# A written-out order of 3128 jobs is replaced by another one

## The chip, the cores and the metric

The kernel runs on one core of one Trainium2 chip. The metric is the device time of one execution in microseconds (us); a kernel's figure is the median of several runs. One further execution was recorded by the hardware profiler, and all rows below come from that one. A core has five engines with queues of their own that are worked off in order: TensorE (PE in the rows; PEld is its weight load), VectorE (DVE), ScalarE (ACT), GpSimd (POOL) and SyncE (SP), which here issues nearly all transfers. All transfers that SP issues run on the same 16 DMA engines.

## The reference

Eight batches, eight heads, 576 positions, 64 numbers per head. Rotary embedding on q and k, softmax attention, and then a gated feed-forward stage on the attention's output x (8 x 576 x 512):

```python
q_rot, k_rot = (rotate(q), rotate(k))
scores = scale * np.matmul(q_rot, k_rot.transpose(0, 1, 3, 2))
scores = scores - np.max(scores, axis=-1, keepdims=True)
attn = np.exp(scores)
attn = attn / (np.sum(attn, axis=-1, keepdims=True) + 1e-09)
x = np.matmul(attn, v)            # then heads side by side: B, S, 512
...
for k in range(5):
    gate_pre += conv_w[k][None, None, :] * xp[:, k:k + S, :]   # xp: x behind 4 zero rows
gate = 1.0 / (1.0 + np.exp(-gate_pre))
val = x @ w_val
return (gate * val @ w_out).astype(np.float32)
```

## The kernel before

Two heads form a pair, so there are 32 pairs, p = 0 to 31, and four pairs make a batch. Products of full precision are made of three TensorE products of rounded parts: a high part `hi` and a rest `lo` (hi*hi, hi*lo, lo*hi). A pair goes through these steps, each of which is one or several jobs:

- `load`, `load_v`: SP brings q (`qin`), k (`kin`) and v from memory. `qin` and `kin` exist once, so the next pair's load waits until the pair ahead has been turned into `q` and `k`.
- `rope_mul`, `rope_add` (DVE or POOL), `qk_hi`, `qk_lo`: the rotation and the two parts. For pair 0 alone the addition is done by TensorE (`rope_mm`, L314), with the identity and a swap matrix as weights.
- `s_mm` (L364), `s_mix` (L374): scores of 128 query rows into a bank of PSUM. For the first four pairs (`APART`) each head has its own job.
- `s_max` (DVE, L389) and `s_exp` (ACT, L398): the row maximum, and the exponential with the row sum.
- `t_mm` (PE, L384): the probabilities are transposed in blocks of 64; `t_copy` (ACT or DVE, L467, L469) takes them out of PSUM into `pt` and `pr`.
- `r_add`, `r_inv`, `r_copy`, `r_write`, `r_read`: the reciprocal row sums are written to memory (`rd`, L526) and read back spread over all partitions (`rb`, L534, three transfers of 288 KB in all).
- `pv_mm`, `pv_left` (PE, L480, L490): attention times v. `x_norm` (DVE, L538) multiplies the result with `rb`, which gives x.
- `x_hi`, `x_lo`, five `tap`s (L567 to L570) and `gate` (L582): the parts of x, and the gate.
- For each batch `f_mm` (PE, L602) with w_val, then `y_mul`, `y_hi`, `y_lo`, then `f_mm` with w_out, `o_out` (ACT L637 or DVE L638) into one of two places of the buffer `o`, and `o_dma` (SP, L641), which sends 288 KB of it out. The next `o_out` into the same place waits until that transfer has ended.

PSUM has four units (`u`), each of two banks. Every job that starts a new result in PSUM names its unit, and waits until the last reader of what stood there is done.

Nothing is decided while the kernel runs, and nothing by a scheduler when it is built. The function lists the 3128 jobs with the engines that may do each and with what each reads and writes. The text `ORDER` (lines 33 to 158) then names them one after the other: the job's number; behind it V, A or G where it may run on DVE, ACT or POOL; behind a colon the buffers and PSUM units it takes; and with `<` a job that it has to follow. `Plan.run` calls them in that order, and each engine's queue holds its own jobs in that order. `FILLS` (line 159) says at which place of the order a number of transposes of the identity is put in, whose result nobody reads:

```python
            if step in FILLS:                  # L205
                fill(*FILLS[step])
...
    def fill(n, slot):
        bank = psum.tile([128, 2, 512], F32, name="ps_f", tag=f"u{slot}")
        for _ in range(n):
            T.transpose(out=bank[:, 0, 0:128], in_=ident, identity=ident)   # L405
```

Of the kernel before, what the change touches and what calls it, by code (L numbers as in the profile page):

```python
# [33 lines left out]
7 24 8 11 17 0:0 35 10 153 113 229 30V 12V 13V 18V 14:0 19V 31V 20:1 25V 15 26V 9 104 16 32:2 36V 21 140 114A 37G 27:3 22 1 33 115 38:0 28 29 116 45:1  # L34
39 34 23 117 119A 42:3 40 46:0 48:2 43:1 147 142G 47:0 51:0 49:2 44:1 57:1 141V 105A 41 54:3 52:3 50 143G 58:0 53 120V 144A 74:2 55:1 59:2 66:0 145V
56:3 63:1 148V 216 75A:0 72:3 149V 82A:0 76:2 146 150V 73A:0 67<148 64:2 151A 60:3 106 65 152 77A 61:3 160:1 223 218G 68:0 62 163:2 217V 69 83:3 161:1
84A 70 219G 80 71 154:0 162:0 164:2 118 85 165:1 172:1 107 87:0 86A 169:2 81A 88:0 155:3 220A 78:3 224G 173:0 156 170:1 174:2 157:0 221V 171:3 166:1
158:2 292 225G 222 175:2 89:0 159 167:3 121V 168 178:0 226V 79A 131 184:1 2 227V 185A:1 186:3 228 179<2 187A:1 3 176:0 236:1 299 294G 180:1 177 233:3
4 237:2 293G 181 239:2 234:3 194A:1 238:0 230:0 5 182 240:0 235:1 190:1 295V 132A 92:3 231:1 296A 133 90 232 297V 241 93 6 300V 488 377:100 298 301V
110A 91 191A 183 108 188:0 134 302V 197:2 254:1 189A 192 109 195 303V 262:0 198A 193A 490V 255<198 199:1 196A 94 304 263A:0 242:2 256:2 495 489G 378A  # L40
95 251:0 270A:0 257 243:3 111G 245:3 252:1 244:2 248:1 246:0 491G 253:3 315:2 249:2 247 260:0 135 250 379 321:3 316:3 112G 261A:0 266:1 322:1 492A
202:0 258 497V 122 317:0 203 200:1 259 136 323:1 268:2 496V 267A 271 273 312:3 380 275:0 274A 498V 269A 276:0 309:1 201:1 272A 381 383A 264:2 313:0
493G 137A 204 310:2 265A 382 205 560 499A 138V 311 327:2 500 494 314:2 384V 567 306:1 328:3 96A:0 385G 206 123A 307:1 318:3 329 124 368:011 207 308
561G 277:0 324:2 319:2 330:0 210A:1 325:0 562G 320:3 211 305 326 336:3 125 331<211 208A:1 212 278:2 563G 337A:1 213 279 346A:1 369A 569G 214 340:3
564A 332:3 215:0 280 370 98A:1 139V 281 371 333 99 374A 338:0 334 341A 126 372 282 100 375G 339A:1 342:3 335 573 101 343A 347:0 568G 349 283 102 348A
502:23 351:1 350A 352:1 373 103:1 344 503:1 376G 345A 505:2 504:0 353:1 512:10 570V 506:2 513:0 565G 571A 517:23 515:3 514:1 520:1 209G:2 395:013 501
128A 632 356:1 516:3 518:2 354 129V 521 572 519 507:03 127 284A:2 639 357 286A:2 510:0 130G 508:3 355 511 633G 287 509 358 288 396A 530:3 97G:4 359
522:0 531A:0 289 528:1 538V:0 634V 529A:0 523<538 290 635G 574:31 524:1 291:2 566 534:2 577:2 525 641G 575:0 578:0 539:0 536 535V 576:2 526 532:1
285G:0 527 533A 540V 579:32 397 360V:3 541 636A 546:1 580:3 640G 543:0 537A 544:0 547 582:1 581 542V 637V 583 584:03 398 704 362A:2 548 545:0 585:2
361G:1 363 549 586:1 587:0 642G 550 364 588:3 600:0 365 717 643A 426:3 399 427 601A:1 366 706G 428 551 429 367:3 594:0 644 589:12 610A:1 400 638 711  # L50
430<610 401A 590:3 431 705G 595<610 592:1 591 432 433 596:2 593 402G 415:1 434 416 597 606:2 435V 707G 604:0 607A:1 436 417 418 598 605A 403V 646:23
599 713V 708A 611:0 608 613 649:0 419<599 709G 612A 420 615:1 647:3 650:1 421 616:1 422 614V 648:3 712V 860 404:3 405 386:013 609A 423 714G 406 617:1
407 424A 651:20 710 425 715A 408<710 654:1 409 410 652:2 655 411 602:1 862G 653 412 603A 413V 666:0 861G 674:2 414 682A:0 667<682 675A:0 716 661:13
387A 668:0 620:2 867 863G 664:3 669 621 662:1 665:0 388 663:2 656:03 389 552A:4 390 672:1 392A 659:2 618 864A 657:0 660 619 391 673A:0 622 868G 658
718:31 623 670 393G 723:02 719:3 721:1 720:1 865G 724:2 722:3 437:3 671 438 726:0 725 678:1 932 869V 727 873 680:0 683 645 679V 685 870G 676:2 687:0
686A 688:0 439 684V 677A 440 681V 744:1 871V 733:02 745A:1 872 441<871 734:3 442 939 933G 443 736:1 735:0 444 738:1 737:2 934G 445 689:0 446A 728:02
935G 447 739<446 731:2 692:3 729:0 394G 732 690 740:3 730 693 941G 554V:2 741 555 748:0 754A:1 742 556 940G 746:1 749A 691 557 747A:1 558 694 942G
559:4 874:01 695 866 943A 468:2 936V 458:3 877:1 937G 459 743 460 878:1 875:2 461 944 469 876:3 1004 752:1 470 696A:0 1011 626V:0 471 624A:1 462<696
627 757 755 463 758A 628 464 756A 759:1 465 760:1 629 472<758 466A:0 473 630 474 1006G 467 750:3 753V 631:2 761:1 475 938 751V 879:10 697G:4 476A:1
882:0 889:23 477 1005G 880:3 883 890:1 881 900:0 1007G 892:2 891:0 894:1 901V:0 893:2 902:2 1012G 910V:0 903A:0 884:30 895<910 1013G 885:0 762:2 887:3  # L60
886 764 896:1 1014G 698A:3 765 897 699 625G:2 763 1015A 700 888 701 1008A 951:10 702 1009G 766 703:0 954:2 478:3 952:0 1017 955:1 898 479 1076 899 480
# [884 lines left out]
```

## Time and profile before

| | |
|---|---|
| median of 3 runs (lowest, highest) | 695.08 us (694.02, 696.48) |
| the profiled execution | 694.14 us |
| its span, first to last instruction | 692.4 us |
| PE busy | 658.4 us, 95% |
| DVE busy | 572.9 us, 83% |
| ACT busy | 467.0 us, 67% |
| POOL busy | 303.1 us, 44% |
| granted TensorE clock, mean over the span | 0.979 of full speed |
| moved by DMA | 72.85 MB, mean 105 GB/s |

Busy time counts matmuls, arithmetic and copies, not waiting. An engine that is busy for 95% of the span can lose little by waiting, but it can also be busy at half its clock. The granted clock is given as a share of 2.4 GHz; it has two levels, 1.2 and 2.4 GHz. Figures between them are means over a stretch.

### The profile page before, as it was taken

How to read it: one execution, taken by the hardware profiler on the slowest of the kernel's cores; microseconds unless marked ns; L12 is line 12 of the kernel's file. 1: busy time of each engine (PE TensorE's matmuls, PEld its weight loads, DVE VectorE, ACT ScalarE, POOL GpSimd, SP SyncE). 2: the span in 40 equal slices, each digit the busy share in tenths (PEclk: the TensorE clock that was granted, in tenths of full speed). 3: DMA queues.
4: the chain of work that ended last, by engine and by line, in shares of the span. 5: the costliest groups of instructions: out<-in, count | busy, mean ns of one | idle time of the engine just before them, and what ended most of it. 6: DMA issues, size and time to landing. Idle time of an engine off the chain costs nothing. (4 is left out here: it accounts for less than half of the span.)

```text
span 692.4 us, 21271 instructions
## 1 busy us (share of the span) xinstructions
PE 658.4 (95%) x8967; PEld 542.8 (78%) x8967; DVE 572.9 (83%) x868; ACT 467.0 (67%) x1004; POOL 303.1 (44%) x241
## 2 busy tenths in 40 slices
PE   9999899999999989999989998999999999999997
PEld 8877568787888867967877767878779788679796
DVE  5999999999889887887887877688878878888673
ACT  4889988877577776677776666666576654777511
POOL 1325666577533256537325554236555370450000
PEclk9689999999999999999999998999999999999999
DMA  7264434243334222334323323322344232231102
GB/s 237 89 181 142 138 99 141 88 132 110 122 104 142 77 101 88 105 111 138 121 88 108 108 70 104 87 79 84 123 123 138 93 126 68 63 99 37 54 19 69
DMA packets 42721, 72.85 MB, mean 105 GB/s; under 512 B 15449, under 2 KB 18050, under 8 KB 42626
## 3 DMA queue, kind: packets, MB, share of 16 engines
q1 hardware_dynamic: 42082, 70.91, 32.3%
q8 instruction: 70, 1.15, 0.7%
q10 hardware_dynamic: 544, 0.59, 0.3%
q14 instruction: 25, 0.20, 0.1%
HBM read 61.89 MB, written 9.59 MB: 103 GB/s over the span
## 5 line engine op out<-in xcount | busy, mean ns | idle before, releaser
L389 DVE TENSOR_REDUCE nm<-ps_s 128x1 f32<-128x576 f32 x288 | 206.5, 750 | 42.0 <-PE ps_s L364 29.6
L398 ACT ACTIVATE p<-ps_s,nm 128x576 f32<-128x576 f32 x256 | 187.9, 739 | 76.4 <-DVE nm L389 74.1
L364 PE MATMUL ps_s<-k,q 64*128 64x288 f32 x1536 | 155.7, 312 | 8.3 <-ACT o L637 2.9
L364 PEld LDWEIGHTS ps_s<-k,q 64*128 64x128 f32 x1536 | 129.0, 191 | 31.4 <-ACT p L398 8.8
L480 PE MATMUL ps_a<-pt,v 128*64 128x256 f32 (+1 forms) x1024 | 137.3, 412 | 2.2 <-ACT p L398 0.6
L301 POOL TENSOR_TENSOR kin<-kin,tab 128x576 f32<-128x576 f32 x49 | 70.7, 1452 | 131.7 <-DMA kin<-in_k 99.1
L467 ACT COPY pt<-ps_t 128x1024 f32<-128x1024 f32 (+1 forms) x119 | 110.5, 945 | 24.4 <-PE ps_t L384 22.9
L602 PE MATMUL ps_f<-y,wout_hi 64*128 64x288 f32 (+2 forms) x1024 | 110.7, 302 | 3.8 <-DVE x L538 1.9
L567 DVE SCALAR_TENSOR_TENSOR ps_c<-x,cw,ps_c 128x576 f32<-128x576 f32 (+2 forms) x132 | 105.7, 802 | 5.7 <-ACT ps_c L570 2.0
L480 PEld LDWEIGHTS ps_a<-pt,v 128*64 128x64 f32 x1024 | 69.0, 137 | 49.5 <-issue 4.8
L384 PE MATMUL ps_t<-ident,p 64*128 64x64 f32 x2172 | 97.9, 229 | 6.8 <-ACT p L398 2.9
L384 PEld LDWEIGHTS ps_t<-ident,p 64*128 64x128 f32 x2172 | 87.4, 141 | 20.5 <-ACT p L398 8.3
L602 PEld LDWEIGHTS ps_f<-y,wout_hi 64*128 64x128 f32 x1024 | 83.8, 185 | 10.0 <-DVE x L538 2.8
L301 POOL TENSOR_TENSOR qin<-qin,tab 128x640 f32<-128x640 f32 (+1 forms) x43 | 65.8, 1537 | 57.9 <-DVE nm L389 23.5
L602 PE MATMUL ps_f<-xh,wval_hi 64*128 64x288 f32 (+2 forms) x512 | 86.5, 316 | 3.5 <-ACT p L398 1.5
L602 PE MATMUL ps_f<-xh,wval_lo 64*128 64x288 f32 (+2 forms) x512 | 81.0, 294 | 0.0
L602 PE MATMUL ps_f<-xl,wval_hi 64*128 64x288 f32 (+2 forms) x512 | 80.9, 294 | 0.0
L602 PE MATMUL ps_f<-y,wout_lo 64*128 64x288 f32 (+2 forms) x512 | 79.2, 291 | 0.0
L602 PEld LDWEIGHTS ps_f<-xh,wval_hi 64*128 64x128 f32 x512 | 53.8, 187 | 8.2 <-ACT p L398 2.3
L336 POOL TENSOR_TENSOR k<-kin,k 128x576 fp32r<-128x576 f32 x26 | 37.0, 1423 | 52.0 <-ACT k L327 17.5
L552 POOL TENSOR_TENSOR xl<-x,xh 128x576 fp32r<-128x576 f32 (+1 forms) x26 | 36.4, 1400 | 46.3 <-ACT xh L546 32.2
L602 PEld LDWEIGHTS ps_f<-xl,wval_hi 64*128 64x128 f32 x512 | 53.8, 187 | 0.0
(108 smaller groups left out, 922.5 us busy)
## 6 DMA issues: line engine op xcount, KB each, us to landing
kin<-in_k SPq DMA_DIRECT2D x31, 576.0 KB
qin<-in_q SPq DMA_DIRECT2D x31, 512.0 KB
v<-in_v SPq DMA_DIRECT2D x32, 320.0 KB
out_t<-o SPq DMA_DIRECT2D x28, 288.0 KB
rb<-rd SPq DMA_DIRECT2D x31, 144.0 KB
rb<-rd SPq DMA_DIRECT2D x31, 128.0 KB
wst<-in_w_val SPq DMA_DIRECT2D x4, 512.0 KB
o<-in_w_out SPq DMA_DIRECT2D x4, 512.0 KB
```

The source lines that it names most:

```text
L301: return eng.tensor_tensor(out=t[:, i, a:b], in0=t[:, 0 if p < RAW else i, a:b], in1=table[:, i, a:b], op=ALU.mult)
L336: return eng.tensor_tensor(out=lo, in0=rotated(p, n, a, b), in1=hi.bitcast(F32), op=ALU.subtract)
L364: T.matmul(out=tiles[h][:, half, 0:288], lhsT=st["q"][HEAD[h], x, c * 128:c * 128 + 128], rhs=st["k"][HEAD[h], y, k0 + half * 288:k0 + hal ...
L384: T.transpose(out=bank[0:src.shape[1], x, k * D:(k + 1) * D], in_=src[rows], identity=ident[rows, rows])
L389: return V.tensor_reduce(out=st[f"nm{i}"], in_=st[f"s{i}"], axis=AX.XY, op=ALU.max, negate=True)
L398: return A.activation(out=to.rearrange("p (b x) -> p b x", b=2), in_=st[f"s{i}"], func=AF.Exp, bias=st[f"nm{i}"], scale=1.0, accum_out=sum ...
L467: return A.copy(out=dst, in_=src)
L480: T.matmul(out=st[f"a{g}"][HEAD[h], 0:n], lhsT=st["v"][:, j, h, :], rhs=st[f"pt{g}"][:, h * 4 + j], start=(j == 0), stop=False)
L552: return eng.tensor_tensor(out=st["xl"][:, a:b], in0=xs[p % NX][:, 4 + a:4 + b], in1=st["xh"][:, a:b].bitcast(F32), op=ALU.subtract)
L567: return V.scalar_tensor_tensor(out=acc, in0=x_sb, scalar=w, in1=acc, op0=ALU.mult, op1=ALU.add)
L602: inst = T.matmul(out=acc[:, x, 0:hi - lo], lhsT=wt[w][HEAD[h], kc, dc * 128:(dc + 1) * 128], rhs=mv[HEAD[h], lo:hi], start=(turn == 0 and ...
```

## The change

The table `ORDER` is replaced by another one, and `FILLS` with it. Jobs, buffers, arithmetic and number of transfers are the same; the place of nearly every job in the order, the engine of some jobs that have a choice, and many buffer and PSUM unit numbers differ. The new table comes from a planner that let transfers queue behind each other. The identity transposes at the start are 20, not 50, and stand three places earlier in the order.

```diff
 ORDER = """
-7 24 8 11 17 0:0 35 10 153 113 229 30V 12V 13V 18V 14:0 19V 31V 20:1 25V 15 26V 9 104 16 32:2 36V 21 140 114A 37G 27:3 22 1 33 115 38:0 28 29 116 45:1
...
 """
-FILLS = {15: (50, 0)}
+FILLS = {12: (20, 0)}
```

How often a step that has a choice runs on which engine, before and after: `t_copy` on DVE 72 and 64 (ACT 184 and 192), `rope_mul` on POOL 92 and 92, `qk_lo` on POOL 26 and 21 (DVE 41 and 46), `tap` on DVE 146 and 143 (ACT 19 and 22), `y_hi` on DVE 15 and 11 (ACT 21 and 25), `x_hi` on DVE 11 and 14 (ACT 22 and 19), `weight_step` on POOL 9 and 14 (DVE 39 and 36).

Three places of the queues show what moves. The first is TensorE's queue behind the identity transposes and the rotation of pair 0, where `ps_s` are scores, `ps_t` transposed probabilities and `p` the probabilities; before:

```order
L364 MATMUL ps_s<-k_71,q_73 128x288 x36
L384 MATMUL ps_t<-ident,p 128x64 x16
L384 MATMUL ps_s<-ident,p 128x64 x4
L374 MATMUL ps_s<-k_71,q_73 128x288 x6
L364 MATMUL ps_s<-k_71,q_73 128x288 x6
```

and TensorE's queue at the same place now:

```order
L364 MATMUL ps_s<-k_71,q_73 128x288 x48
L384 MATMUL ps_s<-ident,p 128x64 x4
L374 MATMUL ps_s<-k_71,q_73 128x288 x6
L384 MATMUL ps_t<-ident,p 128x64 x16
L374 MATMUL ps_s<-k_71,q_73 128x288 x6
```

All 48 score matmuls of the first pair's four query tiles now stand ahead of its first transposes, where 36 did.

The second place is DVE's first work on pair 0, the products of `qin` and `kin` with the table `tab` (L301) and the rests `k` (L336) and `q` (L333); before:

```order
L301 TENSOR_TENSOR qin<-qin,tab 128x256
L301 TENSOR_TENSOR kin<-kin,tab 128x288 x4
L301 TENSOR_TENSOR qin<-qin,tab 128x256
L301 TENSOR_TENSOR qin<-qin,tab 128x128 x2
L336 TENSOR_TENSOR k_71<-ps_r,k_71 128x288
L301 TENSOR_TENSOR qin<-qin,tab 128x256
L336 TENSOR_TENSOR k_71<-ps_r,k_71 128x288
```

and DVE's queue at the same place now:

```order
L301 TENSOR_TENSOR kin<-kin,tab 128x288 x3
L301 TENSOR_TENSOR qin<-qin,tab 128x128
L301 TENSOR_TENSOR kin<-kin,tab 128x288
L301 TENSOR_TENSOR qin<-qin,tab 128x128
L301 TENSOR_TENSOR qin<-qin,tab 128x256 x4
L657 TENSOR_SCALAR o<-o 128x20
L333 SCALAR_TENSOR_TENSOR q_73<-ps_r,q_73 128x128
L660 TENSOR_SCALAR o<-o 128x20
L661 SCALAR_TENSOR_TENSOR o<-o 128x20
L336 TENSOR_TENSOR k_71<-ps_r,k_71 128x288 x2
```

DVE now makes all ten products (one of them was POOL's) before the first rest, and those of `kin` come first.

The third place is SP's queue of transfers around the loads of pair 23, where batch 3 leaves through `out_t`; before:

```order
L293 DMA qin<-in_q 128x2x512
L293 DMA qin<-in_q 64x2x64 x2
L289 DMA kin<-in_k 128x1152
L641 DMA out_t<-o 128x576
L526 DMA rd<-rr 9x128
L641 DMA out_t<-o 128x576
L293 DMA qin<-in_q 128x2x512
L293 DMA qin<-in_q 64x2x64 x2
L289 DMA kin<-in_k 128x1152
L534 DMA rb<-rd 64x576
```

and SP's queue at the same place now:

```order
L293 DMA qin<-in_q 128x2x512
L293 DMA qin<-in_q 64x2x64 x2
L641 DMA out_t<-o 128x576
L289 DMA kin<-in_k 128x1152
L297 DMA v_75<-in_v 128x640
L526 DMA rd<-rr 9x128
L293 DMA qin<-in_q 128x2x512
L293 DMA qin<-in_q 64x2x64 x2
L526 DMA rd<-rr 9x128
L289 DMA kin<-in_k 128x1152
L297 DMA v_76<-in_v 128x640
L534 DMA rb<-rd 64x576
```

The first output now stands ahead of the load of `kin`, not behind it.

## Rows read from the trace of the kernel before

**Rows 1.** The page: busy time by engine, and TensorE's clock in 40 slices.
```profile
PE 658.4 (95%) x8967; PEld 542.8 (78%) x8967; DVE 572.9 (83%) x868; ACT 467.0 (67%) x1004; POOL 303.1 (44%) x241
...
PEclk9689999999999999999999998999999999999999
```

**Rows 2.** Windows: length, busy PE, PEld, DVE, ACT, POOL, then clock, DMA share, GB/s.
```profile
0.00:20.00 20.00, 17.81 (x128) 16.01 (x130) 12.51 (x33) 9.64 (x24) 4.25 (x9) 0.97 0.70 221
20.00:40.00 20.00, 19.24 (x182) 18.38 (x180) 17.35 (x29) 16.39 (x38) 6.12 (x5) 0.60 0.42 117
...
80.00:100.00 20.00, 17.22 (x212) 12.75 (x214) 19.95 (x30) 17.09 (x38) 13.60 (x11) 0.93 0.41 125
```

**Rows 3.** Timeline of PE: start, duration, work, [wait ahead of it and its end].
```profile
245.74 0.34 PE L384 MATMUL ps_s<-ident,p 64*128 64x64 f32 x4 [1.02 <-DVE o L638]
...
267.28 0.53 PE L602 MATMUL ps_f<-y,wout_hi 64*128 64x288 f32 x4 [1.15 <-DVE x L538]
...
351.80 1.06 PE L364 MATMUL ps_s<-k,q 64*128 64x288 f32 x12 [0.82 <-DVE x L538]
...
413.60 0.71 PE L384 MATMUL ps_t<-ident,p 64*128 64x64 f32 x16 [0.74 <-DVE x L538]
...
429.07 1.81 PE L364 MATMUL ps_s<-k,q 64*128 64x288 f32 x11 [2.94 <-ACT o L637]
...
452.03 3.02 PE L480 MATMUL ps_a<-pt,v 128*64 128x256 f32 x24 [0.60 <-DVE x L538]
...
497.04 0.54 PE L602 MATMUL ps_f<-y,wout_hi 64*128 64x288 f32 x4 [0.79 <-DVE x L538]
```

**Rows 4.** Timeline of SP and ACT from 418 us, around the longest wait.
```profile
418.62 2.69 SPq L293 DMA_DIRECT2D qin<-in_q  x3
...
421.36 0.59 SPq L289 DMA_DIRECT2D kin<-in_k  x1
...
421.99 0.43 SPq L641 DMA_DIRECT2D out_t<-o  x1
...
428.37 0.65 ACT L637 ACTIVATE o<-ps_f 128x576 f32<-128x576 f32 x1 [2.69 <-DMA out_t<-o]
```

**Rows 5.** Windows with the columns of rows 2: stretches at the slow clock.
```profile
19.38:26.20 6.82, 6.82 (x71) 6.80 (x68) 5.91 (x10) 6.17 (x13) 0.53 (x1) 0.55 0.26 86
...
29.62:39.86 10.24, 10.24 (x98) 9.77 (x98) 8.50 (x14) 7.81 (x19) 3.46 (x3) 0.53 0.41 106
...
428.98:435.80 6.82, 6.73 (x62) 6.73 (x64) 1.77 (x3) 3.12 (x10) 5.96 (x5) 0.55 0.13 46
```

**Rows 6.** Timeline from 402 us: row sums of one pair written, read, used.
```profile
405.31 0.51 SPq L526 DMA_DIRECT2D rd<-rr  x1
...
407.88 1.75 SPq L534 DMA_DIRECT2D rb<-rd  x3
412.79 0.76 DVE L538 TENSOR_TENSOR x<-ps_a,rb 128x576 f32<-128x576 f32 x1 [1.84 <-DMA rb<-rd]
```

**Rows 7.** Timeline of the first 16 us, PE and DVE.
```profile
1.36 7.49 PE L405 MATMUL ps_f<-ident 128*128 128x128 f32 x50 [1.36 <-POOL ident masks.py:199]
...
4.38 0.42 DVE L301 TENSOR_TENSOR qin<-qin,tab 128x256 f32<-128x256 f32 x1 [2.97 <-DMA tab<-in_tab]
...
8.90 0.75 PE L314 MATMUL ps_r<-kin,ident 128*128 128x288 f32 x2
...
10.62 0.46 DVE L336 TENSOR_TENSOR k<-ps_r,k 128x288 fp32r<-128x288 f32 x1 [2.44 <-ACT k L327]
...
13.34 2.60 PE L364 MATMUL ps_s<-k,q 64*128 64x288 f32 x24
```

**Rows 8.** Timeline of the last pair: its attention on PE, its x on DVE.
```profile
656.79 0.76 PE L490 MATMUL ps_a<-pr,v 64*64 64x320 f32 x8
...
658.16 0.42 DVE L538 TENSOR_TENSOR x<-ps_a,rb 128x256 f32<-128x256 f32 x1
```

More of the change, by code (lines that the diff above doesn't have):

```diff
@@ L38 @@
[L38 to L49, printed above, removed]
@@ new lines @@
+1305G 1063 1096:2 1099 927 1065 1097 1306G 928 1066 929 1110:2 930 850:3 1126A:1 851 1067 852 931:1 853 1307V 1238 1111<1126 1100:10 996V:4 1112:0
+997G:3 854<996 1103:1 855 1113 856 1101:3 1104 857 840:2 1308V 1102 841 1070V:0 1309G 842 1315A 858V:1 1120:1 843 1071 1114 1121A 1376 1118:3 1115
+1072 844<1115 1119A:1 1122:1 1073 845 1123A 846 1316 847 1074 1246:31 848A:0 1068A:0 820:2 849 1249:2 821 1075:2 1383 1378G 822 1247:0 1250:1 823
+1248:2 1251:01 1377G 1310 1317 1129:3 824<1310 1252:1 1131:1 825 1130A 1132:1 1379G 826 1254:3 1253 1124 1127 827 1255 1128V 1272:0 828V:0 1125A
@@ new lines @@
+1706:3 1713 1718:2 1831V 1707 1667 1716:3 1719A:1 1824V 1767:01 1825V 1717A:1 1542:2 1770:0 1714 1543 1544 1768:2 1771:0 1545 1832 1769:3 1762:31 1715
+1983 1729:0 1546<1715 1763:1 1731:1 1547 1724 1765:3 1764 1727 1548 1725V 1732:1 1549 1826 1766 1790:3 1728V 1550 1730A 1788:1 1791A:0 1551V 1722:0
+1789A:0 1720:3 1552 1733:1 1723A 1721V 1772:21 1985G 1782:0 1773:0 1553:3 1976 1984G 1775:2 1554 1774:1 1555 1783<1775 1776:2 1556 1986G 1784:1
+1777:21 1798V:0 1785 1557<1798 1780:3 1558 1559 1778:0 1781 1560 1779 1839:01 1561 1786 1734:2 1562A 1977G 1840:2 1736 1563 1841:0 1978G 1842:1
@@ new lines @@
+2333 2605A 2617 2615 2315 2726 2334 2616A 2316A:1 2335 2797V 2610:2 2618A 2619:1 2608:3 2620:1 2611V 2317 2338:0 2609A 2339 2340 2336V:0 2341 2798
+2621:1 2486A:2 2558A:3 2624:1 2487 2625 2488 2864 2805 2622 2489 2337 2623 2559 2871 2626 2560 2342<2558 2490 2343 2627 2491:3 2344 2345 2561 2318:1
+2630A:2 2319 2346V:1 2628A:2 2320 2631 2321 2347 2629G:3 2669:0 2877 2632 2670 2671 2562 2672 2322<2632 2633 2323 2563:0 2324 2634 2325 2872G
+2673<2563 2326V:0 2674 2635:4 2675 2676 2865G 2734:32 2677 2658:1 2678A 2737:0 2659 2660 2679 2738:1 2661 2866V 2739:02 2735:3 2867G 2742:2 2736:2
@@ new lines @@
+2980:0 2995 2977A:1 2974:2 2714<2995 2981A 2975V 2715 2716 2717 2996:1 2986:0 2930V:2 2997:0 2931 2928A:0 3000:1 2998:0 2987A 2929G:1 2932 3002
+2718V:0 3003 2999 2933 3001 2934 3004 2935:0 2719 3005 3006 3010V:0 3008A:1 3009V:2 3007 3011 3016A 3018A:3 3038:2 3039 3040 3041 3024:1 3025 3012
+3026 3017V 3027 3019 3042<3012 3043 3020 3044 3013 3045 3014 3028<3020 3029 3021 3015:2 3030 3022 3052:0 3053 3046 3023 3031 3054 3032 3066:3 3049
+3033A 3055 3050V 3067 3034 3068 3035 3047V 3069 3048 3056<3035 3036V 3057 3037 3058 3051 3092:1 3093 3070<3037 3094 3095 3059 3071 3060 3072 3063
@@ L158 @@
+3061A 3073 3064V 3096<3060 3062 3097 3098 3065 3099 3074 3080:2 3102V:1 3081 3077 3082 3103 3083 3078A 3116:0 3100A:0 3079 3075A 3117 3101 3076
+3084<3075 3085 3086 3087 3118 3088A:1 3119 3089 3104:1 3090V:0 3105 3120<3090 3091 3121 3122 3123 3106 3124A:1 3107 3125 3126A:0 3108<3126 3127 3109
+3110 3111 3112V:1 3113 3114V:0 3115
 """
-FILLS = {15: (50, 0)}
+FILLS = {12: (20, 0)}
 class Plan:
```

216 lines of the change are left out of this document (105 added, 111 removed).

## The prediction

> **What bounds the kernel now.** I read the page's busy times first, then windows of 20 us, then every wait of PE of 0.2 us or more, and then, for the longest of them, what SP had issued ahead. The page says that PE is busy for 658.4 of 692.4 us, so that all its waiting together is 34.0 us, and that its clock falls in a few slices only [rows 1]. So the matmuls set the time, they are the same after the change, and a new order can win three things: waits of PE, slow-clock time, and the two ends of the program. The windows show one exception: from 80 to 100 us DVE is busy for 19.95 of 20 us and PE for 17.22, so the first stretch, in which PE has no work of an earlier batch to fill in, is set by DVE as well [rows 2].
>
> The waits of PE are many and short. Seven of them lead back to a transfer [rows 3]: at 267.28, 413.60, 452.03 and 497.04 PE waits for x, and x waits for the row sums `rb`; at 351.80 the releaser named ahead of x is a transposition that x does not need, so I count that one too; at 245.74 and 429.07 PE waits for a PSUM unit that an output `o` still has to leave, because `o`'s place has not been sent yet. They add up to 1.02 + 1.15 + 0.82 + 0.74 + 2.94 + 0.60 + 0.79 = 8.06 us. The longest shows the mechanism: the output is issued at 421.99 behind 576 KB of `qin` (418.62) and 576 KB of `kin` (421.36), and the next user of its place goes on at 428.37, 6.4 us after the issue [rows 4]. When PE starts again at 429 its clock is at the lower level until 435.80 [rows 5].
>
> **Part by part.** The sum is made against the profiled execution, 694.14 us; the median of runs is 695.08, 0.94 more.
>
> *Transfers that queue.* For each transfer I took from both orders the PE work that lies between its issue and the step that needs it, with the durations of PE's groups in the trace (an estimate, since PE also waits), and what SP issues in the 3.5 us ahead. For the five waits for x (pairs 12, 16, 19, 21, 23) that was 4.6, 5.2, 4.6, 8.2 and 5.8 us behind 1476, 292, 4, 320 and 1184 KB; now it is 4.6, 8.2, 6.1, 7.1 and 4.9 us behind 324, 4, 324, 320 and 0 KB. For the two outputs it was 4.0 us behind 1472 KB and 4.2 us behind 1152 KB; now it is 5.3 us behind nothing and 4.6 us behind 576 KB. The queue shown above has the second of these: `out_t` ahead of `kin` and no longer behind it. I take all seven as gone: -8.06 us. If the clock does not fall behind the longest, the 6.82 us from 428.98 on, half of whose pulses were missing, give back 3.41 us [rows 5].
>
> *What is late next.* Ten reads of row sums still have less than 6 us of PE work until x (4.1 to 5.9 us); before there were ten as well, four of which held PE up, for 0.88 us on average (pairs 12, 16, 19 and 23). Four times 0.88 is +3.5 us; the ends are 0 and 8.8 (all ten), and I take 3.5 because a read takes long even without a queue: with one load and its own write ahead, pair 19's is issued at 407.88 and x starts at 412.79, 4.9 us later [rows 6]. The Trainium skill, page "DMA: Bandwidth & Descriptors", section on the anatomy of one DMA, fits 2.0 us plus the bytes at 436 GB/s, which would be 2.7 us (an estimate from that page) for these 288 KB. By that rule no read of the ten would be late and the total below would be 3.5 us lower; the trace's 4.9 us speaks against it, and the measurement decides. For the outputs that still have a short lead I add 0.5 us (0 to 2.94, the longest wait before).
>
> *Cover of arithmetic.* The new order pays for its transfers elsewhere. Of PE's 1113 steps that read what DVE, ACT or POOL made, 79 had less than 1.5 us of PE work between the producing step and them; now 94 have. Seven of the 15 are transposes of the left-over column block straight behind the reciprocal of the row sums. PSUM units taken over with no PE work since their last reader's step go from 74 to 87 of 550. The waits that are left, 34.0 - 8.06 - 1.36 (the first transposes wait so long for the identity [rows 7]) = 24.6 us, are 0.31 us for each of 79 steps; 15 more would be +4.7 us. Not all of the 24.6 us hangs on these steps, so I take half of it, 2.5; the lower end is -2, should the planner have put the short leads where the producers are early.
>
> *The start.* Fifty transposes run from 1.36 to 8.85 us, and the first rotation matmul follows at 8.90 [rows 7]. Twenty end at about 1.36 + 20 x 0.15 = 4.4. The table's first half lands at 4.38 [rows 7], `kin`'s first products are now DVE's first, and the rotation can begin near 5.4. DVE makes ten products by about 9.5 and two rests of k by 11.3; the first scores needed them and began at 13.34 [rows 7]. So up to 2.0 us can be won, DVE's wait of 2.44 us for the first rest with it. Against that, PE now pauses between the rotation matmuls and has 48 score matmuls in a row ahead of it. Twenty-four took 2.60 us at the full clock [rows 7], so 48 take 5.2 us, and 10.4 us at half. The ends are -2.0 and +5.2; I take 0, since the trace shows 17.1 us at half speed already from 19.38 on [rows 5], and since DVE, not PE, is the limit by 80 us [rows 2].
>
> *The end.* Before, eight feed-forward steps of batch 6 (3.4 us of PE) stood behind the last pair's attention; now all are ahead of it. The attention ends at about 657.5 and x of the last pair starts at 658.16 [rows 8]. Now PE has the rest of that product and three steps, 1.5 us, until it needs the first x parts, which take DVE some 2 us (0.42 for x [rows 8], a tap and a rest of about the same length, and the hand-overs). With one more such place behind the gate I take +1.0 us (0 to 2).
>
> *At nothing.* The moves between engines take some 6 us off DVE's 572.9 us and add some 8 to ACT's 467.0 [rows 1]; both have room over the whole span, and inside the first 100 us DVE's work up to the first feed-forward step differs by 1 us. Without that room ACT's 8 us would be the price. POOL is idle for more than half of the time.
>
> Sum: -8.06 - 3.41 + 3.5 + 0.5 + 2.5 + 0 + 1.0 = -4.0 us, that is 690.2 for the profiled execution and **691.1 us** for the median.
>
> **The rivals.**
> 1. *The planner's gain comes out whole.* The ten reads and the outputs hold nobody up (-4.0) and the start wins its 2.0 us: 691.1 - 6.0 = 685.1. For it: of the ten short reads none now stands behind more than 576 KB issued just ahead, and four did before. Against it: pair 19's 4.9 us without such a queue [rows 6].
> 2. *No change in the end.* The transfers' waits turn into waits for PSUM and for ACT: the cover costs its 4.7 us, and the reads 5.4 in place of 3.5 (six of ten late): 691.1 + 2.2 + 1.9 = 695.2. For it: PE's other waits, three times as long in total, are of this kind. Against it: single waits of this kind are short.
> 3. *Slower: the start falls into the slow clock.* With 30 fewer transposes and pauses behind them PE stays at 1.2 GHz where it now has the full clock, from 5.7 us to 19.38 and from 26.20 to 29.62. All of the first 39.86 us at half speed would be 17 us more of it, half of which is lost: +8.5, and 691.1 + 8.5 = 699.6. It decides from 4.0 / 0.5 = 8 us of added slow time on (no gain left), and from 12 us on the kernel is slower. For it: the clock fell at 19.38 although PE was busy for 17.81 of the first 20 us [rows 2, 5]. Against it: 48 score matmuls in a row are dense work, and a part of the loss hides behind DVE. The Trainium skill, page "TensorE: Matmul & The Clock Gate", part 1, has the slow clock as the default that sustained activity releases. By that rule this rival gains weight, since the transposes are such activity; the trace's slow stretches at 29.62 and 428.98, behind pauses, agree.
>
> **How the numbers follow.** A difference of 0.3%, 2.1 us, is about what a measurement of this kernel can tell from none, so faster is below 693.0 and slower above 697.2. I give the forecast (687 to 693) 0.43, rival 1 (below 687) 0.17, rival 2 (693 to 697.2) 0.17 and rival 3, with a worse cover than in rival 2, 0.23. So faster has 0.60, same 0.17, slower 0.23. The range, 683 to 699, holds rival 2, most of rival 1 and nearly all of rival 3 and leaves out about 0.2.
>
> **What would show it.** Right, if no wait of PE of over 1.2 us ends with an `o` or an x behind `rb`, if the clock holds from 100 us to the end, and if the first scores start before 12 us. The reads' term is wrong if PE's waits for x add up to under 1 or over 6 us. The cover's term is wrong if PE's remaining waits are not between 24 and 30 us. The forecast is wrong if the slow clock of the first 40 us changes by more than 5 us, or if a new long wait stands where none was.

## The result and the profile after

The new order takes **674.10 us** (median of 4 runs, 672.66 to 675.39) against 694.98 (median of 4, 694.02 to 696.48) for the old one: a ratio of 0.9697, 95% interval 0.9668 to 0.9726, or 20.9 us less. The forecast was 691.1, faster by 4, with a range of 683 to 699. The direction was right and the size was missed fivefold. The profiled execution of after is the slowest of its four, 675.39 us with a span of 673.6; against the 694.14 of before that is 18.75 us less.

The page of after, busy times and clock, answers to [rows 1]:

```profile
PE 648.9 (96%) x8937; PEld 534.9 (79%) x8937; DVE 559.3 (83%) x858; ACT 474.8 (70%) x1016; POOL 299.9 (45%) x239
...
PEclk9799979999999999999999999999999999999999
```

PE's idle time falls from 34.0 to 24.7 us. That is 9.3 of the 18.8 us. Its busy time falls by 9.5 us as well. Of that 3.5 us are the 30 identity transposes that are left out (50 took 7.49 us [rows 7], 20 take 3.97), which are also the 30 matmuls fewer on the page, and an estimated 1.7 us are less time at the slow clock (below). The remaining 4.3 us are time that the page counts as busy and that PE spends on the same matmuls. So idle time was not all the time that PE lost.

Where it comes from shows in windows of 100 us. The columns are those of [rows 2]; first before, then after:

```profile
100.00:200.00 100.00, 97.29 (x1392) 80.22 (x1392) 91.85 (x134) 75.46 (x160) 60.81 (x46) 1.00 0.37 118
200.00:300.00 100.00, 95.55 (x1386) 78.73 (x1384) 82.37 (x119) 69.60 (x148) 45.95 (x37) 1.00 0.32 100
300.00:400.00 100.00, 95.64 (x1346) 77.41 (x1346) 83.39 (x118) 70.71 (x153) 47.11 (x37) 1.00 0.35 109
400.00:500.00 100.00, 93.79 (x1277) 76.65 (x1276) 78.57 (x113) 63.95 (x139) 43.20 (x33) 0.97 0.30 95
```

```profile
100.00:200.00 100.00, 96.69 (x1409) 79.69 (x1410) 88.75 (x133) 78.19 (x168) 59.39 (x48) 1.00 0.37 116
200.00:300.00 100.00, 98.70 (x1430) 81.94 (x1431) 86.23 (x124) 71.76 (x155) 53.31 (x42) 1.00 0.33 104
300.00:400.00 100.00, 99.32 (x1426) 81.54 (x1424) 86.33 (x126) 75.08 (x162) 44.16 (x35) 1.00 0.35 110
400.00:500.00 100.00, 98.66 (x1420) 80.77 (x1418) 82.37 (x122) 72.55 (x154) 53.61 (x42) 1.00 0.35 110
```

From 200 to 500 us PE was idle for 4.45 + 4.36 + 6.21 = 15.0 us and now is for 1.30 + 0.68 + 1.34 = 3.3. The starts of DVE's L538, which makes x of each pair, tell the same. In after x of pair 0 starts 8.8 us earlier, of pair 3 it starts 5.4 us later (96.77 against 91.35), at pair 11 the two are level, then the distance grows: -7.8 us at pair 19 (405.00 against 412.79), -13.1 at pair 20, -20.1 at pair 22 (464.10 against 484.22), and -16.5 at the last. Behind it another 2.2 us are won up to the end of the span.

The longest waits of PE in after, apart from the first one for the identity, in the columns of [rows 3]:

```profile
78.14 0.46 PE L384 MATMUL ps_t<-ident,pm 64*128 64x64 f32 x8 [1.11 <-ACT pt L467]
82.08 1.05 PE L364 MATMUL ps_s<-k,q 64*128 64x288 f32 x11 [1.48 <-ACT g L582]
...
139.45 0.40 PE L602 MATMUL ps_f<-xh,wval_hi 64*128 64x288 f32 x2 [0.77 <-ACT p L398]
...
256.97 1.05 PE L364 MATMUL ps_s<-k,q 64*128 64x288 f32 x11 [0.78 <-ACT pt L467]
```

None of them ends with an x or an `o`. The waits for x that the timeline lists add up to 0.34 us (4.86 before), those for `o` on ACT and DVE to 0.81 (4.63 before).

The tightest output and pair 19's row sums in after, from the timeline of SP, ACT and DVE, answer to [rows 4, 6]:

```profile
395.83 0.51 SPq L526 DMA_DIRECT2D rd<-rr  x1
...
398.84 1.75 SPq L534 DMA_DIRECT2D rb<-rd  x3
...
405.00 0.75 DVE L538 TENSOR_TENSOR x<-ps_a,rb 128x576 f32<-128x576 f32 x1
...
411.35 0.34 SPq L641 DMA_DIRECT2D out_t<-o  x1
411.79 1.88 SPq L289 DMA_DIRECT2D kin<-in_k  x1
...
416.39 0.76 DVE L638 TENSOR_SCALAR o<-ps_f 128x576 f32<-128x576 f32 x1 [0.22 <-PE ps_f L602]
```

The read of the row sums is issued 9.0 us earlier than before (407.88) and x waits for nothing behind it. The output is issued ahead of `kin`, no longer behind it, and the next user of its place goes on 5.0 us later without waiting for it.

The waits on DMAs, all engines; engine, line and what it waited for: us in all, times, longest. First before, then after:

```profile
POOL kin L301 <- DMA kin<-in_k: 99.1, 17, 11.7
DVE x L538 <- DMA rb<-rd: 9.6, 6, 2.2
POOL qin L301 <- DMA qin<-in_q: 7.4, 5, 3.9
ACT o L637 <- DMA out_t<-o: 6.3, 2, 3.6
```

```profile
POOL kin L301 <- DMA kin<-in_k: 35.9, 7, 9.5
POOL qin L301 <- DMA qin<-in_q: 34.3, 11, 9.7
...
DVE x L538 <- DMA rb<-rd: 3.1, 2, 1.8
```

ACT no longer waits for an output at all. POOL, which turns q and k by their angles, waits 36 us less for loads. In the old order that wait was the largest of all on a DMA, and the prediction did not count it, because POOL is idle for more than half of the time.

The start in after, PE, answers to [rows 7]:

```profile
1.36 3.97 PE L405 MATMUL ps_f<-ident 128*128 128x128 f32 x20 [1.36 <-POOL ident masks.py:199]
5.62 0.72 PE L314 MATMUL ps_r<-kin,ident 128*128 128x288 f32 x2 [0.30 <-PE ps_f L405]
...
11.04 1.43 PE L364 MATMUL ps_s<-k,q 64*128 64x288 f32 x12
12.88 3.49 PE L364 MATMUL ps_s<-k,q 64*128 64x288 f32 x15 [0.41 <-ACT q L327]
```

The first scores start 2.3 us earlier. The stretches at the lower clock (1.2 GHz) in after answer to [rows 5]; there is none from 93.35 us to the end:

```profile
14.85:21.68 6.83, 6.83 (x47) 6.49 (x46) 5.78 (x11) 5.65 (x15) 4.23 (x3) 0.50 0.08 23
28.50:35.33 6.83, 6.83 (x42) 5.35 (x42) 5.34 (x10) 5.30 (x16) 2.65 (x2) 0.50 0.34 113
83.11:93.35 10.24, 9.00 (x49) 6.41 (x50) 9.40 (x15) 8.54 (x22) 7.20 (x6) 0.50 0.49 143
```

The third one stands behind the two longest waits above and in the stretch that DVE sets. Before has a shorter one near there, 3.41 us from 97.27 on, which [rows 5] do not list. The one of before at 429 us is gone. All slow stretches together are 27.3 us before and 23.9 after, and half of the difference, an estimated 1.7 us, is what the clock gives back on balance.

### The profile page after: what moved, and what is told of

Its sections match the earlier page's. It is cut to its first block, busy times and chain, and to the rows that moved or that the text cites. A ratio compares the mean times of both kernels' runs of the same rounds, so it can differ in the third digit from the quotient of the medians.

```text
span 673.6 us, 21213 instructions
## 1 busy us (share of the span) xinstructions
PE 648.9 (96%) x8937; PEld 534.9 (79%) x8937; DVE 559.3 (83%) x858; ACT 474.8 (70%) x1016; POOL 299.9 (45%) x239
## 3 DMA queue, kind: packets, MB, share of 16 engines
q8 instruction: 70, 1.15, 0.7%
## 4 chain that ended last, share of the span: by engine, by line
PE 75%; DVE 9%; ACT 9%; DMA 4%; issue 2%; SPq 1%; DVEq 0%; ACTq 0%
PE ps_f L602 26%; PE ps_a L480 18%; PE ps_s L364 15%; PE ps_t L384 9%; PE ps_s L374 4%; ACT p L398 3%; DVE nm L389 3%; ACT pt L467 3%; PE ps_a L490 2%; DVE ps_c L567 1%; DMA rb<-rd 1%; DMA wst<-in_w_val 1%; DMA tab<-in_tab 1%; PE ps_s L384 1%; DMA qin<-in_q 1%
## 5 line engine op out<-in xcount | busy, mean ns | idle before, releaser
L364 PE MATMUL ps_s<-k,q 64*128 64x288 f32 x1536 | 160.2, 312 | 8.3 <-ACT pt L467 2.9
L364 PEld LDWEIGHTS ps_s<-k,q 64*128 64x128 f32 x1536 | 131.8, 191 | 31.6 <-ACT p L398 12.4
L480 PE MATMUL ps_a<-pt,v 128*64 128x320 f32 (+1 forms) x1024 | 139.6, 418 | 0.3 <-ACT p L398 0.2
L467 ACT COPY pt<-ps_t 128x1024 f32<-128x1024 f32 (+1 forms) x125 | 114.8, 941 | 19.3 <-PE ps_t L384 18.2
L301 POOL TENSOR_TENSOR kin<-kin,tab 128x576 f32<-128x576 f32 x52 | 73.4, 1421 | 91.6 <-DMA kin<-in_k 35.9
L384 PE MATMUL ps_t<-ident,p 64*128 64x64 f32 x2172 | 94.7, 225 | 3.2 <-ACT p L398 1.5
L384 PEld LDWEIGHTS ps_t<-ident,p 64*128 64x128 f32 x2172 | 85.7, 139 | 13.2 <-ACT p L398 7.8
L301 POOL TENSOR_TENSOR qin<-qin,tab 128x640 f32<-128x640 f32 x40 | 62.1, 1562 | 64.2 <-DMA qin<-in_q 34.3
L602 PEld LDWEIGHTS ps_f<-xh,wval_lo 64*128 64x128 f32 x512 | 54.7, 184 | 0.0
L552 POOL TENSOR_TENSOR xl<-x,xh 128x576 fp32r<-128x576 f32 x25 | 35.6, 1424 | 41.7 <-ACT xh L546 32.9
```

The lines of the kernel that those rows point to most:

```text
L301: return eng.tensor_tensor(out=t[:, i, a:b], in0=t[:, 0 if p < RAW else i, a:b], in1=table[:, i, a:b], op=ALU.mult)
L364: T.matmul(out=tiles[h][:, half, 0:288], lhsT=st["q"][HEAD[h], x, c * 128:c * 128 + 128], rhs=st["k"][HEAD[h], y, k0 + half * 288:k0 + hal ...
L384: T.transpose(out=bank[0:src.shape[1], x, k * D:(k + 1) * D], in_=src[rows], identity=ident[rows, rows])
L467: return A.copy(out=dst, in_=src)
L480: T.matmul(out=st[f"a{g}"][HEAD[h], 0:n], lhsT=st["v"][:, j, h, :], rhs=st[f"pt{g}"][:, h * 4 + j], start=(j == 0), stop=False)
L552: return eng.tensor_tensor(out=st["xl"][:, a:b], in0=xs[p % NX][:, 4 + a:4 + b], in1=st["xh"][:, a:b].bitcast(F32), op=ALU.subtract)
```

## The experiments

Eighteen kernels ran, each timed in three rounds beside before on the same chip; ratios are to that before. Where loads are cut or contents replaced, the instructions stay and the output is not the reference's.

**1. Cut the loads, in both orders.** From the third pair on q and k load 64 columns of each part, from the fourth pair on v loads one block of five:

```
-SP.dma_start(out=t[:, i, a:b], in_=k2[p, :, i, a:b])
+SP.dma_start(out=t[:, i, a:b if p < 2 else 64], in_=k2[p, :, i, a:b if p < 2 else 64])
... (q alike)
-SP.dma_start(out=v, in_=v2[p])
+SP.dma_start(out=v[:, 0:5 if p < 3 else 1], in_=v2[p, :, 0:5 if p < 3 else 1])
```

> The order of before; from pair 2 on q and k bring 64 columns of 576 or 512 and from pair 3 on v brings one block of five, so results are wrong from there on, and loads take about an eighth of their bytes. Theory A (transfers that come late, with all that queues behind them on DVE and ACT, cost the old order most of the 21 us): 674 to 681 us. Theory B (only the seven counted waits and one slow stretch hung on transfers, 11.5 us; the rest of the gain is a better order of arithmetic): 683 to 687 us.

> The new order with the same cut in bytes as in the run with the old order. Both theories: 668 to 674 us, since few waits on transfers are left. What tells them apart is the distance to the old order with light loads: A at most 8 us, B 12 us or more.

Old order 678.45 us, 0.9811 (0.9758 to 0.9864), 13.8 us less. New order 671.34 us, 0.9715 (0.9652 to 0.9778), which its ratio with whole loads, 0.9697, does not differ from. So the old order loses some 13 us to transfers and the new one nothing that can be measured, which here means less than some 4 us. Some 7 us between the orders do not go with the bytes of the loads.

**2. Take away what waits for results, in the old order.** x of all pairs but the last is multiplied by the cosine table and not by the row sums that come back; outputs of batches 1 to 6 are sent from that table. Together, then each alone:

```
-in1=state[p]["rb"][:, a:b]
+in1=state[p]["rb"][:, a:b] if p == NP - 1 else table[:, 0, a:b]
-in_=ffn[b, "o", oc, lo])
+in_=ffn[b, "o", oc, lo] if b in (0, NB - 1) else table[:, 0, lo:hi])
```

> The order of before with full loads; x is multiplied with the cosine table in place of the row sums that are read back, and the outputs of batches 1 to 6 are sent from that table, so that nobody waits for these two kinds of transfer (results are wrong). Theory A, if it is these two kinds: 675 to 682 us. Theory B: 683 to 687 us. Theory C (late loads of q and k are what holds the old order up): 686 to 692 us, far above the run with light loads.

> The old order; the outputs of batches 1 to 6 are sent from the cosine table, so that no transfer has to leave before the arithmetic may write the next result into its buffer (their content is then not the result). The row sums are read back as before. The pair of cuts, outputs and row sums, brought 7.3 us. If it is the longest wait (2.94 us, behind ScalarE's o at 429 us) and the slow clock behind it (3.41 us): -5 to -7 us here, and the other half of the pair -0 to -2. If the many small waits behind row sums that come back late carry it: -2 to -3 here and -4 to -6 there.

> The old order; x of all pairs but the last is multiplied by the cosine table, not by the row sums that come back through DRAM, so that x never waits for them (its content is then not the result). The transfers are still issued. Outputs as before. If the longest wait and the slow clock behind it carry the 7.3 us of the pair: -0 to -2 us here. If the waits behind late row sums do (six in the trace, 4.9 us of PE's waits end with x): -4 to -6 us.

Together 684.96 us, 0.9891 (0.9858 to 0.9924), 7.3 us less. Outputs alone 690.84, 0.9945 (0.9926 to 0.9963); row sums alone 689.53, 0.9950 (0.9914 to 0.9985). By the ratios that is 3.8 and 3.5 us, about half each. The theory that the outputs carry it (-5 to -7 us) is at the very end of their interval; the other one (-2 to -3 and -4 to -6) is not excluded. An even split fits best. Two lines of PE's timeline without waits for row sums, the waits for `o` there:

```profile
247.13 0.34 PE L384 MATMUL ps_s<-ident,p 64*128 64x64 f32 x4 [0.94 <-DVE o L638]
...
425.37 1.06 PE L364 MATMUL ps_s<-k,q 64*128 64x288 f32 x11 [0.86 <-ACT o L637]
```

The longest wait of before, 2.94 us [rows 3], is 0.86 here although the output still has to leave: ACT goes on 4.7 us after its issue, behind the same loads, and not 6.4 us after. That the missing waits for row sums did this is not shown: with light v alone (experiment 4), where x waits for its row sums as before, it is 4.9 us. The trace's semaphore records show what differs. Each of these transfers counts its semaphore up 16 times, as its parts land. Fifteen parts of this output had landed 4.5 us after the issue in before and 4.5 us here, 4.8 with light v. The sixteenth landed 1.8 us behind them in before, and at most 0.1 us behind them in the other two. What delayed it is not settled.

**3. All cuts together, in both orders.** Experiments 1 and 2 in one kernel.

> The old order with both cuts together: loads of q, k and v cut short from the third or fourth pair on (as in the run with light loads, 13.8 us faster than the chip's before less some microseconds of the order), x of all pairs but the last multiplied by the cosine table, and the outputs of batches 1 to 6 sent from that table. What is left in it is the old order of the arithmetic with hardly a transfer to wait for. If row sums and outputs were late only behind the loads, light loads had cured them too: 0.978 to 0.983 of before, as with light loads alone. If they add to it, 0.970 to 0.977.

> The new order with the same cuts of loads, row sums and outputs. The distance to the run before it is what the order of the arithmetic is worth with no transfer in play. If the 7 us that were left with light loads are the order of the arithmetic: again 5 to 8 us faster than the old order with the same cuts, 0.965 to 0.972 of before. If they were waits for row sums and outputs that light loads had not taken away: within 2 us of it.

Old order 679.49, 0.9817 (0.9790 to 0.9844); new order 671.24, 0.9698 (0.9674 to 0.9722). Once the loads are light, taking away the result waits as well adds nothing that can be measured (0.9811 and 0.9817): row sums and outputs were late only behind the loads. And 8.2 us remain between the orders. Transfers are not wholly out of play in them: POOL still waits for `kin` for 44.3 us in the old order and 17.2 in the new one, and no run takes that away.

**4. Which load.** Only q and k cut, then only v.

> The old order, only the loads of q and k cut to 64 columns from the third pair on (from 576 KB each to 64 KB); v whole. If results and v queue behind the big loads of q and k, which carry 1.15 MB of a pair's 1.47: most of the 13.8 us, 0.979 to 0.985 of before. If it goes by the loads that are late themselves and v is the tighter one, 0.985 to 0.995.

> The old order, only the loads of v cut to one block of five from the fourth pair on (320 to 64 KB). If what queues behind the big loads carries the gain, v is a fifth of the bytes: 0 to -3 us. If v itself is late for its products: -4 to -10 us.

q and k: 680.92, 0.9821 (0.9788 to 0.9854). v: 690.51, 0.9972 (0.9941 to 1.0002). So q and k, 1.15 of a pair's 1.47 MB, carry it. The timeline of SP and ACT with light q and k, at the place of [rows 4]:

```profile
413.78 2.26 SPq L293 DMA_DIRECT2D qin<-in_q  x3
416.08 0.61 SPq L289 DMA_DIRECT2D kin<-in_k  x1
416.73 0.60 SPq L641 DMA_DIRECT2D out_t<-o  x1
...
420.72 0.64 ACT L637 ACTIVATE o<-ps_f 128x576 f32<-128x576 f32 x1
```

The queue has the same order as before. With 128 KB of q (the expectation says 64) and 64 KB of k in place of 576 KB each ahead of it, the output's place is free 4.0 us after the issue or earlier, not after 6.4 us, and ACT does not wait; by the semaphore records the last part landed after 2.5 us. From pair 19's x to pair 20's x this kernel wins 6.1 us on before; the prediction's 2.94 us of wait and 3.41 us of clock are 6.35. But light v alone, at 0.9972 in all, wins 4.9 us there, so a good part of it comes and goes with the late part of that one output.

The rest, 5 to 6 us between the cut of result waits (7.3 us) and all cuts (13.4 us), is put down to loads of q and k that are late themselves by elimination. One such place shows in before, in the chain of work that ended last; start, duration, what, of some of its steps:

```profile
525.00 5.58 DMA kin<-in_k
...
530.74 1.43 POOL kin L301
...
538.00 0.69 ACT k L327
...
543.73 0.66 ACT g L582
...
544.43 0.40 PE ps_t L384 x6
```

The load reaches PE through POOL, ACT and DVE, and what PE waits for last is a gate. POOL's waits for `kin` go along with the times in the old order, 99.1 us in before, 98.2 without result waits, 53.2 here and 44.3 with all cuts, but they are no price: with light v they are 74.9 us and hardly anything is won, and in the new order light loads bring POOL's waits for q and k from 70.2 to 27.7 us without a measurable gain.

**5. The queue's order alone, and the arithmetic's alone.** The first kernel has all instructions of PE, DVE, ACT and POOL in the old order and the DMAs of SP in the new one, as far as the old arithmetic allows (16 had to stay behind others); the second is the reverse (10 had to stay). The order of SP is moved by moving the entries of its jobs in the table; at the start of the first, for instance (names of the jobs in place of their numbers):

```
-... load_v 1, load_weight val 1, load_v 2, load_weight val 0, load k 1, load q 1, load_v 0 ...
+... load_v 1, load_weight val 1, load_weight val 0, load k 1, load q 1, load k 2, load_v 0 ...
```

> The instructions of TensorE, VectorE, ScalarE and GpSimd stand in the old order, with the old buffers; only the DMAs of SyncE are issued in the new order, as far as the old arithmetic allows (16 of them had to stay behind others). Theory A, that the order of the queue itself brings the transfers' share of the gain (13.8 us by the run with light loads): 0.97 to 0.985 of before, the waits behind x and o in the trace mostly gone. Theory B, that transfers are late because the arithmetic frees their buffers or makes their sources late, and that the queue must be ordered with the arithmetic: within 0.4% of before or slower (an old queue slot that suited the old arithmetic is given up), with new waits of ScalarE, VectorE or GpSimd on DMAs.

> The reverse: all arithmetic in the new order with its new buffers, and the DMAs of SyncE in the old order, as far as the new arithmetic allows (10 had to stay behind others). Theory A: the transfers' share of 13.8 us is lost again, about 688 us, 0.985 to 1.0 of before. Theory B: it keeps more than half of the gain, 0.965 to 0.98 of before. The four kernels (old and new arithmetic, old and new queue) then say how much each part brings alone and how much only both together.

> The old arithmetic with the new order of SyncE's DMAs (60 us slower than before), and the loads of q, k and v cut as in the first run. If the 60 us are transport (loads that carry their bytes at the wrong time): most of it goes, within 10 us of the old order with light loads. If they are entries of one queue that wait for arithmetic and hold back those behind them: over 40 us of it stay.

Both mixtures are far slower than either pure kernel: 754.79 us, 1.0870 (1.0825 to 1.0916), and 728.92, 1.0501 (1.0466 to 1.0536). Theory A falls, and theory B was too mild. The longest waits of PE in the first:

```profile
376.52 1.81 PE L364 MATMUL ps_s<-k,q 64*128 64x288 f32 x11 [8.35 <-ACT o L637]
...
571.33 0.61 PE L602 MATMUL ps_f<-xh,wval_hi 64*128 64x288 f32 x2 [7.23 <-ACT o L637]
665.04 1.11 PE L384 MATMUL ps_t<-ident,p 64*128 64x64 f32 x16 [8.36 <-DVE x L538]
```

They end with `o` and x, as the waits of before did, three times as long. With light loads as well it takes 718.22 us, 1.0366 (1.0324 to 1.0407), 40 us over the old order with light loads. So light loads win some 37 us here and 14 in the old order, and of the 61 us 40 stay. PE's longest waits are again behind `o` and x (6.61, 6.37 and 4.91 us), as they would be if entries of one queue waited for arithmetic and held back those behind them; no run shows that apart. Part of the loss is the clock, which in the first mixture fell during the three waits shown (372.24 to 382.48, 566.80 to 577.04 and 658.96 to 669.20 us are at the lower level). Its mean is 0.945 in the profile of the first mixture and 0.948 in that of the second, 0.979 in before. The span times the share missing from full speed is, as an estimate, 41, 38 and 15 us, so up to 27 of the 61 us and 23 of the 35.5.

**6. The choice of engine.** 260 steps that the two orders give to different engines change engine, with light loads. Each entry of the table keeps its place and its buffers and gets the other table's letter.

> The old sequence and buffers with light loads, but each of the 260 steps that the new order gives to another engine runs on that engine. If the choice of engine alone carries the gain of arithmetic (VectorE gets about 8 us less): 3 to 6 us faster than the old order with light loads, 0.972 to 0.977 of before. If a choice of engine only serves the sequence that it was made for: slower than the old order with light loads, 0.985 to 1.02.

> The reverse: the new sequence with light loads and the old engine choices. If the choice alone carries the gain: 0.976 to 0.982 of before, as the old order with light loads. If it serves its own sequence: slower than that, 0.985 to 1.02.

731.52 us, 1.0574 (1.0535 to 1.0614), and 731.36, 1.0563 (1.0513 to 1.0614): 53 and 60 us slower than the same sequence with its own engines. The choice of engine is part of the sequence too. The pages of the old sequence with light loads, first with its own engines, then with the new ones:

```profile
span 676.5 us, 21271 instructions
...
PE 650.5 (96%) x8967; PEld 534.4 (79%) x8967; DVE 564.7 (83%) x868; ACT 466.8 (69%) x1004; POOL 302.6 (45%) x241
```

```profile
span 730.0 us, 21270 instructions
...
PE 670.5 (92%) x8967; PEld 544.3 (75%) x8967; DVE 563.0 (77%) x858; ACT 474.4 (65%) x1016; POOL 304.8 (42%) x239
```

DVE has 1.7 us less to do and PE waits 33.5 us more (59.5 for 26.0); PE's busy time rises by 20 us for the same matmuls. Its clock tells most of that: the mean is 0.974 for 0.992, by the same estimate 14 us.

**7. VectorE's cover.** Light loads in both orders, and the third and fourth of the five taps cut to 8 columns.

```
+if k in (2, 3):
+    acc, x_sb = (acc[:, :, 0:8], x_sb[:, :, 0:8]) if b - a == S else (acc[:, 0:8], x_sb[:, 0:8])
```

> The old order with light loads, and of each pair's five taps of the convolution the third and fourth are cut to 8 columns (VectorE does about 50 us less of its 559; the result is then not the convolution's). If the 7 us between the orders with light loads are cover, that is TensorE reached work that VectorE had not finished, both orders come closer to what TensorE needs and the distance to the next run shrinks to under 3 us. If they lie in how TensorE's own groups follow each other, the distance stays 5 to 8 us.

> The new order with light loads and the same two taps cut. Cover: within 3 us of the old order with the same cuts, and little faster than the new order with light loads alone (0.965 to 0.97 of before). TensorE's own order: 5 to 8 us faster than the old one.

673.18 us, 0.9719 (0.9695 to 0.9744), and 670.09, 0.9678 (0.9656 to 0.9700). DVE does 33 us less (531.7 for 564.7), not the 50 expected. The old order gains 5.3 us, the new one 1.3, and their distance shrinks from 7 or 8 us to 3.1. So about 4 us of it were TensorE arriving at work that VectorE had not finished.

**8. The first transposes.** 50 of them in the new order, 20 in the old one (FILLS).

> The new order with 50 identity transposes at the start in place of 20. If fewer transposes won time at the start: 676 to 678 us (the rotation begins 3.3 us later). If they cost a warm clock: 668 to 672 us. If DVE sets the first 100 us in any case: 673 to 676 us.

> The old order in full, with 20 identity transposes at first in place of 50. If the start is part of what the new order gains without transfers: -2 to -5 us. If the number of first transposes hardly matters, as in the new order (675.6 against 674.1 us): within 1.5 us of before.

675.60 us, 0.9755 (0.9708 to 0.9803) against 0.9697 with 20, and 694.14, 1.0031 (0.9992 to 1.0070). Their number alone wins nothing in the old order; in the new one 20 may be worth up to 4 us, but the intervals overlap.

No kernel that computes the reference's result is faster than the new order, and even with all transfers cut that order stands at 0.9698.

## Why the prediction was wrong

The right cause, in too small a size, was joined to two prices that were not paid. By the experiments the 20.9 us are about 13 of transfers (old order with all cuts 0.9817; new order with and without them 0.9698 and 0.9697) and 8 of arithmetic (0.9817 to 0.9698). The prediction had -7.5 and +3.5 for them, the end included. So of the 17 us that it missed, some 12 are a cost of arithmetic that was a gain, and 5 are transfers sized too small. (By arithmetic I mean here what remains between the orders with all cuts; late entries of SP's queue can be part of it.)

*Transfers that queue, -8.06 and -3.41: right in the mechanism.* The seven waits are gone, no long wait stands in their place and the clock holds from 93 us on. Taking away by hand what waited brought 7.3 us of the 11.5. The largest price, 6.35 us at one place, rests in part on luck: 1.8 us of that output's 6.3 us are its one late part. The clock gave back 1.7 us on balance, not 3.41, since 83.11 to 93.35 us is slow now. The wait at 452.03 hangs on pair 20, whose x starts at 451.22, and not on pair 21.

*What was missing from it.* Another 5 to 6 us (0.9891 to 0.9817) go with the bytes of k and q beyond these waits; by elimination, and by the chain above, they are loads that are late themselves. They reach PE through POOL, ACT and DVE, and where such a wait ends, PE's timeline names ACT or DVE and not a DMA. I sorted PE's waits by their last releaser and so counted only transfers that stand one step away. The row that I passed over was POOL's 99.1 us of waiting for `kin`. One rival is untested: with light loads DVE is busy for 8.2 us less with the same instructions (572.9 and 564.7), by the rate of experiment 7 an estimated 1.3 us.

*What is late next, +3.5 and +0.5: failed.* PE's waits for x came to 0.34 us, under the 1 us that was set as its refutation. Transfers cost the new order nothing that can be measured. DVE still waits for two reads, 3.1 us in all, and PE has other work meanwhile. I had priced ten reads at the mean wait of those that held PE up before, because pair 19's x started 4.9 us after the issue with one load ahead [rows 6]. By the semaphore records the reads of three transfers take 3.6 to 7.3 us from the first issue to the last landing in before, half of them at most 3.9, and 3.6 to 6.1 in after, half of them at most 4.0. Pair 19's took 4.8 in before, with one part 1.2 us behind the other fifteen; in after it took 4.0, and x came 6.2 us after the issue. So most reads are shorter than the leads of 4.1 to 5.9 us that I called short. The estimate of 2.7 us from the Trainium skill, page "DMA: Bandwidth & Descriptors", section on the anatomy of one DMA, would have left the term out, and the time agrees with leaving it out, but not with the estimate: that section fits one transfer issued by GpSimd, these are three issued by SP, and no read here takes less than 3.6 us.

*Cover of arithmetic, +2.5: the step that failed most, in sign as well.* PE's waits left were to be 24 to 30 us if it was right; all its idle time but the first wait is now 24.7 - 1.4 = 23.3, those that the timeline lists 17.9 (before, without the seven, 18.0). So no new waits were paid, and with all cuts the new order was 8 us faster. The count of steps with a short lead in PE work (79 to 94) said nothing of how early the producer is. What did change is the producer: I put 6 us less work on DVE at nothing, and it was 13.6 with whole loads (572.9 to 559.3) and 8.3 with light ones (564.7 to 556.4), largest in the copies of transposed blocks (L469, the form named `pt`: 41 of them in 43.1 us before, 35 in 37.2 after). In the old order 33 us less on DVE was worth 5.3 us, so 8.3 us is an estimated 1.3 us by that rate alone. The rest of the 4 us is when DVE does its work, for which no run isolates a cause, nor does one for the 3 us that stay between the orders with a light DVE.

*The matmuls as a fixed sum: failed too.* The prediction said that all of PE's waiting together is 34.0 us of idle time and that the matmuls are the same after the change. The gain stayed below 34.0 us, but half of it was not idle time. PE's busy time is modelled up to the end of a pipelined matmul and covers short pauses between groups. From the start of each PE instruction in the trace, the time from the last start on one line of the kernel to the first start on the next adds up to 112.8 us in before and 94.7 in after (slow-clock stretches counted at full speed). That includes the work of the matmul itself, so only the difference, 18.1 us, speaks. Idle time at these places falls by 11.3 us; the other 6.8 are pauses that the page counts as busy. Within the lines PE takes 1.0 us more, although the 30 transposes are gone, and the clock gives 1.7: 18.1 - 1.0 + 1.7 = 18.8 us.

*The start, 0: about right in time, wrong in its parts.* The first scores came before 12 us, the slow clock of the first 40 us changed by 3.4 us (17.1 to 13.7), so rival 3 did not come. Pair 0 was 8.8 us ahead and pair 3 was 5.4 behind, DVE being the limit there; by pair 11 it was made up. Why pair 3 came late is not settled: the slow stretch from 83.11 us on falls there, with light loads it is 2.0 us late (92.72 against 90.68), and the number of transposes does not decide it (95.89 with 50).

*The end, +1.0: wrong in sign.* From x of the last pair to the end of the span it took 32.7 us (from 659.68) and now 30.6 (from 642.96).

*The signs.* All three signs of being right came true: no wait of over 1.2 us ends with an `o` or an x, the clock holds from 100 us on, and the first scores start at 11.04 us. They ask whether waits are gone and not what that is worth, so they could not tell 691 from 674.

*Rivals.* Rival 1 had the mechanism, the planner's gain whole, and gave 685.1, since it had no term for late loads and none for a gain of cover. It was given 0.17.

## What to carry to other kernels

A wait is traced to a transfer through all the engines between, not by the engine that released last: look at every engine's waits on DMAs, also those of one that is idle half of the time, since what it makes may be needed soon. Their sum is no price; a run with the loads cut short gives one. Idle time of the bounding engine is not all that an order can win where its busy time hides short pauses. And an order is one thing: the queue's order, the sequence and the choice of engine that one planner put together cannot be exchanged piece by piece; each mixture here cost 35 to 61 us, more than the whole gain.

## What was not expected of the hardware

The same 288 KB output behind the same 1152 KB of q and k, in SP's queue, had wholly landed 6.3 us after its issue in before and 6.4 us with 20 transposes, but after 4.6 us without row-sum waits and 4.9 us with light v. With q and k light it was 2.5 us. So the bytes issued just ahead make some 2 us of it, and up to 1.8 us are one of its 16 parts that lands behind the fifteen others; what delays that part is not settled. The mean DMA share, 0.30 to 0.37 in the windows above, tells nothing of it.

The times of before spread from 688.45 to 697.56 us in 63 of the 64 executions beside the experiments (the other took 701.10), against 678.30 to 682.07 in four with light loads. The granted clock goes along with much of this: of the twelve beside experiment 1 the fastest, 689.25 us, had 0.989, and the two slowest, 696.59 and 697.56, had 0.978 and 0.980.

A queue order that does not fit the arithmetic lost 40 us with the loads cut to a small part, and whole loads added some 37 us to that, 23 more than in the old order.
